# Attention scores on diagonal quarters of the array, one sign pass in two on DVE, and a third score buffer

## The chip, the cores and the metric

The kernel runs on one core of a Trainium2 chip. The metric is the time of one launch in device microseconds. Engines are TensorE (PE, with its weight loads PEld), VectorE (DVE), ScalarE (ACT), GpSimd (POOL) and SyncE (SP), which issues most of the DMAs. Each engine works through its own instructions in the order in which the program has them; semaphores tie the engines together.

## The reference

Three layers in a row, on 4 batches of 576 positions and a width of 512.

```python
# 1 attention: 8 heads of 64; heads 0-3 local, heads 4-7 strided
scores = np.matmul(q, k.transpose(0, 1, 3, 2)) / sqrt(64)
mask_local = (rel >= 0) & (rel < 32)
mask_strided = (rel >= 0) & (pos_k % 32 == pos_q % 32)
attn = softmax(where(mask, scores, -1e9));  x = attn @ v
# 2 layer norm and a dense layer, w_ch1 512x2048, w_ch2 2048x512
x = x + np.maximum(xn @ w_ch1, 0.0) @ w_ch2
# 3 one of 8 experts for each token (first layer 512x1024, second 1024x512)
out = p[e] * (np.maximum(x @ w1[e], 0) @ w2[e])
```

The weights of the second layer arrive as 64-bit floats; the kernel makes 32-bit floats of them by bit operations. A softmax row of a local head has 32 keys at most, one of a strided head 18, so only a band of the scores is computed.

## The kernel before

**Stages.** A prologue (to 57 us) computes the attention of batch 0 in an order written out by hand. Then comes a long row of steps of the dense layer, nine chunks of 256 tokens with 16 steps each (to about 615 us); the attention of batches 1, 2 and 3 is spread over its steps 6 to 24, 36 to 54 and 65 to 86, and the first 32 steps alternate between chunks 0 and 1. In those 32 steps the remaining weights are also split. The experts follow.

**Attention.** Two heads are a pair. `prep` transposes queries and keys of a pair on TensorE and copies them to SBUF. Keys lie as kT: 64 rows of head 0 over 64 rows of head 1. Queries lie as qbd: twice as wide, column 2s holds head 0 of position s in rows 0-63 and zeros below, column 2s+1 zeros above and head 1 in rows 64-127. So each half of the rows is copied on its own: in batch 0 the upper one by ACT and the lower one by DVE, later the lower one of the second half by ACT too. A unit is three or four groups of queries (64 for local pairs, 54 for strided ones). `st_scores` makes one product a group, 128 rows by 128 (or 108) query columns as weights against 96 (or 54) keys. In batches 0 and 1 a bf16 product first writes the mask into the bank. Then come the exponentials (ACT), the sum and scaling (DVE), `st_trans` (TensorE transposes, ACT copies to pt) and `st_out` (products with v; each head writes one half of the output partitions, into ps_o). The rows of a unit's scores alternate between the heads, and `st_out` reads every second column of pt. The scaled scores sm have two buffers (SMB) in batches 1 to 3. Of the 48 units 24 are local with three groups, 16 strided with four and 8 strided with three.

**Weights.** The dense layer's weights come in 32 pieces of 128 x 512 values (`load_w`). A piece takes five passes: `w_low` shifts the low words (DVE), `w_sign` writes the sign into the low word and then takes the scaled magnitude of the high word (both ACT), `w_high` joins the two (DVE), and `w_split` makes a high and a low part (ACT and POOL). Consecutive turns do them for consecutive pieces: in turn i the first pass of piece i, the second of piece i-1 and the split of piece i-2. Piece i < 6 (W_START) is worked on in the prologue, the rest in the steps of the dense layer. The calls through `keep` stay in program order; the other order of each engine is the scheduler's, by its own costs.

In the profile an operation of the prologue has line 84, whatever its place in the code. Lines used below: 324 scores, 374 transposes of sm, 382 copy to pt, 392 products with v, 290 to 294 queries, 288 keys, 454 `w_low`, 460 and 461 `w_sign`, 466 `w_high`, 480 and 481 `w_split`, 636 and 638 the first product of a step and its relu h, 639 the remainder of h, 652 the second product.

Of the kernel before, what the change touches and what calls it, by code (L numbers as in the profile page):

```python
# [22 lines left out]
B, H, S, DH = 4, 8, 576, 64  # L23
# [3 lines left out]
STR = 32  # L27
NA = S // STR
# [3 lines left out]
NTT = CT // TT  # L32
WL = 128 + NE + 1
QT = 96
SP = S + 18
GROUPS = (((0, 3), (3, 3), (6, 3)),) * 2 + (((0, 4), (4, 4), (8, 3)),) * 2
QW, KW = (64, 64, 54, 54), (96, 96, 54, 54)
SMW, PTW = 288, 432
# [4 lines left out]
SCALE = 1.0 / DH ** 0.5  # L43
NEG = -1.0e9
Z_THR = -1.5 * 2.0 ** -23


SMB, SM0, PT0, TL = 2, 4, 2, 1
WARM0, WARM, LB = 10, 5, 5
ORD = (((0, 1, 2), (0,)), ((3, 4, 5), (1,)), ((6, 7), (2,)))  # L50
SPANS = ((6, 24), (36, 54), (65, 86))
# [2 lines left out]
W_START, WR, WA, WI, W_DVE = 6, 1.3, 3, 5, 4  # L54
# [16 lines left out]
def attention_moe_moe(ctx: ExitStack, tc: tile.TileContext, q, k, v, g_ln, w_ch1, w_ch2, w_gate, w_local, w1, w2, out):  # L71
# [33 lines left out]
    pool.memset(mean_w, 1.0 / DM)  # L105
    mask_loc = cst.tile([128, 128], F32, name="mask_loc")
    pool.memset(mask_loc, 0.0)
    pool.affine_select(out=mask_loc, in_=mask_loc, pattern=[[-2, 128]], compare_op=ALU.is_ge, fill=-NEG, base=2 * STR, channel_multiplier=1)
    pool.affine_select(out=mask_loc, in_=mask_loc, pattern=[[2, 128]], compare_op=ALU.is_ge, fill=-NEG, base=-1, channel_multiplier=-1)
    mask_str = cst.tile([128, 3, NA], F32, name="mask_str")  # L110
    pool.memset(mask_str, 0.0)
    pool.affine_select(out=mask_str, in_=mask_str, pattern=[[-2 * NA, 3], [-2, NA]], compare_op=ALU.is_ge, fill=-NEG, base=0, channel_multiplier=1)
    pool.affine_select(out=mask_str, in_=mask_str, pattern=[[2 * NA, 3], [0, NA]], compare_op=ALU.is_ge, fill=-NEG, base=2 * NA - 1, channel_multiplier=-1)
    mask_str = mask_str.rearrange("p a b -> p (a b)")

    def high(ap):
# [36 lines left out]
    at_p = at_x.enter_context(tc.tile_pool(name="at_p", bufs=1))  # L153
# [20 lines left out]
        return ps_s["r"].tile(shape, F32, tag="s", name=name)  # L174


    qbds, kTs = [at_p.tile([128, SP, 2], F32, name="qbd")], [at_p.tile([128, SP], F32, name="kT")]
    spare = new_blk([128, 2048], F32, "spare")
    idle = spare[:, 1792:2048].bitcast(BF16)
    qbds.append(spare[:, 0:2 * SP].rearrange("p (s j) -> p s j", j=2))  # L180
    kTs.append(spare[:, 2 * SP:3 * SP])
    for qbd, kT in zip(qbds, kTs):
        pool.memset(qbd[0:64, :, 1], 0.0)
        pool.memset(qbd[64:128, :, 0], 0.0)
        pool.memset(qbd[0:64, S:SP, 0], 0.0)
        pool.memset(qbd[64:128, S:SP, 1], 0.0)
        pool.memset(kT[:, S:SP], 0.0)
    nat, vt, qTs = {}, {}, {}
    xts = {}

# [79 lines left out]
    def prep(b, hp, nm):  # L270

        odd = b == 0 and pairs.index((b, hp)) % 2
        qbd, kT = qbds[odd], kTs[odd]
        qTs[b, hp] = qbd, kT
        for half in range(2):
            t = nat.pop((nm, b, hp, half))
            ps = (ps_m.tile([128, 512], F32, tag="m", name="ps_tr")[:, 0:3 * QT] if b == 0 else side_r([128, 3 * QT], "ps_tr"))
            for i in range(3):
                pe.transpose(ps[:, QT * i:QT * i + QT], t[0:QT, i, :, :].rearrange("p h d -> p (h d)"), ident[0:QT, 0:QT])

            def dst(ap):
                if hp < 2:
                    return ap[:, 3 * QT * half:3 * QT * half + 3 * QT]
                return ap.rearrange("p (r a) -> p r a", a=NA)[:, :, NA // 2 * half:NA // 2 * half + NA // 2]

            s_ = ps if hp < 2 else ps.rearrange("p (a r) -> p r a", r=STR)
            if nm == "k":
                (act.copy if b == 0 else dve.tensor_copy)(dst(kT[:, 0:S]), s_)
            else:
                act.activation(dst(qbd[0:64, 0:S, 0]), s_[0:64], AF.Copy, scale=-SCALE)  # L290
                if half and b:
                    act.activation(dst(qbd[64:128, 0:S, 1]), s_[64:128], AF.Copy, scale=-SCALE)
                else:
                    dve.tensor_scalar(dst(qbd[64:128, 0:S, 1]), s_[64:128], -SCALE, None, op0=ALU.mult)

    sms, pts = {}, {}
    first, units = [], [0, 0]
# [5 lines left out]


    def shape_of(hp, u0):
        return dict(GROUPS[hp])[u0], QW[hp], KW[hp], 2 * QW[hp]

    def mode_of(b, hp):
        return MODES.get((b, hp), MODES.get(b, 0))

    def st_scores(b, hp, u0):
        ng, w, n, m = shape_of(hp, u0)
        ps = side([128, ng, n], "ps_sc")
        qbd, kT = qTs[b, hp]
        mode = mode_of(b, hp)
        mask = lambda i: mask_str[0:m, 0:n] if hp > 1 else mask_loc[:, STR:STR + n] if u0 + i == 0 else mask_loc[:, 0:n]
        if mode:
            cuts = [(0, 1), (1, ng)] if hp < 2 and u0 == 0 else [(0, ng)]
            for lo, hi_ in cuts:
                pe.matmul(ps[0:m, lo:hi_, :], high(ident[0:m, 0:m]), high(mask(lo)).unsqueeze(1).to_broadcast([m, hi_ - lo, n]), start=(lo == 0), stop=False)  # L320
        for i in range(ng):
            q0 = w * (u0 + i)
            k0 = max(0, q0 - STR) if hp < 2 else q0
            pe.matmul(ps[0:m, i, :], qbd[:, q0:q0 + w, :].rearrange("p s j -> p (s j)"), kT[:, k0:k0 + n], start=not mode, stop=not mode or i == ng - 1)  # L324
        if b == 0:
            k = units[0] % SM0 * SMW
            sm = first[0][:, k:k + ng * n]
            units[0] += 1
        else:
            sm = at_p.tile([128, SMW], F32, tag="sm", bufs=SMB, name="sm")[:, 0:ng * n]  # L330
        sm = sm.rearrange("p (g n) -> p g n", g=ng)
        st = at_p.tile([128, 2, 4], F32, tag="st", bufs=5, name="st")
        sms[b, hp, u0] = (sm, st, ps)
        mn = st[0:m, 0, 0:ng]
        if mode:
            new = [lambda: dve.tensor_reduce(mn, ps[0:m], axis=AX.X, op=ALU.min)]
            if mode == 1:
                new.append(lambda: dve.tensor_tensor(sm[0:m], ps[0:m], mn.unsqueeze(2).to_broadcast([m, ng, n]), op=ALU.subtract))
# [30 lines left out]
    def st_trans(b, hp, u0):  # L369
        sm, st, ps = sms.pop((b, hp, u0))  # L370
        ng, w, n, m = shape_of(hp, u0)
        ps = side([128, ng, m], "ps_pt")
        for i in range(ng):
            pe.transpose(ps[0:n, i, :], sm[0:m, i, :], ident[0:m, 0:m])
        if b == 0:
            k = SM0 * SMW + units[1] % PT0 * PTW
            pt = first[0][:, k:k + ng * m]
            units[1] += 1
        else:
            pt = at_p.tile([128, PTW], F32, tag="pt", bufs=2, name="pt")[:, 0:ng * m]  # L380
        pt = pt.rearrange("p (g m) -> p g m", g=ng)
        act.copy(pt[0:n], ps[0:n])
        pts[b, hp, u0] = pt

    def st_out(b, hp, u0):
        ng, w, n, m = shape_of(hp, u0)
        pt, vv = pts.pop((b, hp, u0)), vt.pop((b, hp, u0))
        ps = side([128, ng, w], "ps_o")
        for i in range(ng):
            k = min(w, S - w * (u0 + i)) if hp > 1 else w  # L390
            for j in range(2):
                pe.matmul(ps[64 * j:64 * j + 64, i, 0:k], vv[0:min(n, k) if hp > 1 else n, i, j, :], pt[0:min(n, k) if hp > 1 else n, i, j:2 * k:2], start=True, stop=True)
        o = ps.rearrange("p g q -> p (g q)")
        i = 0
        q0 = w * u0
        nq = min(w * ng, S - q0)
        for c in range(S * b // CT, (S * b + S - 1) // CT + 1):
            base = S * b - CT * c
            if hp < 2:
# [47 lines left out]
    def keep(ins):  # L447

        tc.keep_in_program_order(ins)

    def w_low(i):

        t = stage[i]
        keep(dve.tensor_single_scalar(t[..., 0], t[..., 0], 29, op=ALU.logical_shift_right))  # L454

    def w_sign(i):


# [501 lines left out]
    for n in range(2):  # L960
        i = n * (NE + 129)
# [526 lines left out]
```

## Time and profile before

| | |
|---|---|
| median of 3 runs | 904.97 us (904.07 to 905.69) |
| profiled execution | 902.98 us, its span 901.2 us |
| mean granted clock of TensorE | 0.983 |
| TensorE busy | 867.3 us, 96% of the span |
| DVE, ACT, POOL busy | 474.5, 365.6, 152.2 us |
| prologue / first 32 steps / later steps / experts | to 57 / to about 199 / to about 615 / to the end |

The span is the time from the first to the last instruction. Busy time is that in which an engine executes; a busy TensorE may still work at the lower of its two clock levels, so its busy time is to be read with the granted clock (1.00 is 2.4 GHz). Idle time counts only on the engine that others wait for. The name behind an arrow is the engine whose work ended the wait.

### The profile page before, as it was taken

The numbers are of one execution on the slowest core, as the hardware profiler recorded it, in microseconds if no ns is written. First come the engines' busy times: TensorE is split into PE (matmuls) and PEld (weight loads), VectorE is DVE, ScalarE is ACT, GpSimd is POOL, SyncE is SP. The second block draws the span as 40 slices with busy tenths as digits, with TensorE's granted clock in tenths as the row PEclk, the third lists the DMA queues.
The fourth block names the chain that finished last, engine by engine and source line by source line (L and its number), as shares of the span: only waits on it lengthen the run. The fifth ranks groups of instructions, "written<-read, shape, count | busy, mean of one in ns | idle before, by whom it ended". The sixth has DMA issues, their size and how long they took to land. (4 is left out here: it accounts for less than half of the span.)

```text
span 901.2 us, 17965 instructions
## 1 busy us (share of the span) xinstructions
PE 867.3 (96%) x6668; PEld 777.3 (86%) x6668; DVE 474.5 (53%) x1520; ACT 365.6 (41%) x879; POOL 152.2 (17%) x163
## 2 busy tenths in 40 slices
PE   8989888999999999999999999999999999999995
PEld 5769788999999999999999999999878787787763
DVE  4877775448766546666545555667521233111541
ACT  3688878433455234354211212332122334223550
POOL 2124323211120120120201212020231211110100
PEclk9999999899999999999999999999999999999997
DMA  9836244101212102211000000510663466410730
GB/s 190 250 106 207 59 141 121 50 14 52 65 39 46 48 10 64 47 26 39 1 1 25 1 25 6 207 49 24 239 225 101 150 218 215 139 37 24 291 113 15
DMA packets 95023, 82.91 MB, mean 92 GB/s; under 512 B 67395, under 2 KB 75589, under 8 KB 94920
## 3 DMA queue, kind: packets, MB, share of 16 engines
q1 hardware_dynamic: 87656, 65.41, 24.5%
q0 software_dynamic: 3632, 11.11, 3.7%
q10 hardware_dynamic: 3632, 5.09, 1.6%
q8 instruction: 55, 0.90, 0.4%
q14 instruction: 48, 0.39, 0.1%
HBM read 72.08 MB, written 10.30 MB: 91 GB/s over the span
## 5 line engine op out<-in xcount | busy, mean ns | idle before, releaser
L652 PE MATMUL acc<-h,w 128*128 128x256 f32 x1728 | 247.5, 291 | 1.6 <-DVE h L639 1.5
L636 PE MATMUL ps_h<-xc,w 128*128 128x256 f32 x1728 | 239.6, 287 | 0.0
L652 PEld LDWEIGHTS acc<-h,w 128*128 128x128 f32 x1728 | 220.7, 192 | 5.1 <-DVE h L639 2.5
L636 PEld LDWEIGHTS ps_h<-xc,w 128*128 128x128 f32 x1728 | 221.6, 194 | 1.7
L638 ACT ACTIVATE h<-ps_h 128x256 fp32r<-128x256 f32 x144 | 55.6, 387 | 218.3 <-PE ps_h L636 203.7
L639 DVE SCALAR_TENSOR_TENSOR h<-ps_h,h 128x256 fp32r<-128x256 f32 x144 | 60.6, 421 | 94.2 <-ACT h L638 93.5
L1367 PE MATMUL ps_h<-wx,xs 128*128 128x512 f32 x360 | 87.6, 398 | 0.8 <-DVEq L1294 0.8
L1395 PE MATMUL ps_y<-wx,ht 128*128 128x512 f32 x360 | 87.5, 399 | 0.0
L1367 PEld LDWEIGHTS ps_h<-wx,xs 128*128 128x128 f32 x360 | 66.6, 188 | 15.8 <-DVEq L1294 1.2
L1395 PEld LDWEIGHTS ps_y<-wx,ht 128*128 128x128 f32 x360 | 67.6, 191 | 13.8
L481 POOL TENSOR_TENSOR w<-stg,w 128x512 fp32r<-128x512 f32 x32 | 45.6, 1424 | 120.7 <-ACT w L480 74.5
L1398 ACT ACTIVATE y<-ps_y,pr 128x512 f32<-128x512 f32 x19 | 13.1, 687 | 90.5 <-PE ps_y L1395 54.9
L890 DVE TENSOR_TENSOR xs<-ps_tx,xs 128x512 fp32r<-128x512 f32 x15 | 10.4, 691 | 63.0 <-ACTq L1294 44.8
L1370 ACT ACTIVATE h<-ps_h 128x512 f32<-128x512 f32 x30 | 16.3, 595 | 60.8 <-PE ps_h L1367 60.8
L782 DVE TENSOR_TENSOR wx<-raw,wx 128x1024 fp32r<-128x1024 f32 x32 | 37.5, 1220 | 1.7 <-ACT wx L779 1.3
L460 ACT ACTIVATE stg<-stg 128x512 f16<-128x512 f32 x27 | 37.2, 1377 | 0.6 <-DVE stg L454 0.6
L1399 POOL DMA_INDIRECT out_dram<-y,idx x15 | 15.1, 1007 | 114.6 <-ACT y L1398 66.1
L779 ACT CAST wx<-raw 128x1024 fp32r<-128x1024 f32 x32 | 31.8, 1061 | 5.7 <-PE acc L652 4.1
L354 ACT ACTIVATE sm<-sm,st 108x54 f32<-108x54 f32 (+1 forms) x80 | 27.6, 347 | 13.5 <-DVE st L342 13.4
L1384 DVE TENSOR_TENSOR ht<-ps_th,ht 128x512 fp32r<-128x512 f32 x30 | 19.3, 685 | 24.5 <-ACT ht L1383 24.1
L324 PE MATMUL ps_sc<-kT,qbd 128*108 128x54 f32 (+1 forms) x240 | 30.5, 267 | 0.0
L892 DVE SCALAR_TENSOR_TENSOR pr<-io_e,e_rep,xg 128x8 f32<-128x8 f32 x15 | 3.4, 226 | 51.2 <-ACT y L1398 46.0
(393 smaller groups left out, 1233.7 us busy)
## 6 DMA issues: line engine op xcount, KB each, us to landing
stg<-in_moe_w_ch_dram SPq DMA_DIRECT2D x32, 512.0 KB
raw<-in_moe_w_dram SPq DMA_DIRECT2D x16, 1024.0 KB
raws<-in_moe_w_dram SPq DMA_DIRECT2D x16, 1024.0 KB
xrows<-row ACTq DMA_DIRECT2D x9, 520.0 KB
qnat<-in_q_dram SPq DMA_DIRECT2D x48, 72.0 KB
knat<-in_k_dram SPq DMA_DIRECT2D x48, 72.0 KB
v<-in_v_dram SPq DMA_DIRECT2D x24, 72.0 KB
v<-in_v_dram SPq DMA_DIRECT2D x72, 18.0 KB
```

The costliest lines, as they stand in the source:

```text
L324: pe.matmul(ps[0:m, i, :], qbd[:, q0:q0 + w, :].rearrange("p s j -> p (s j)"), kT[:, k0:k0 + n], start=not mode, stop=not mode or i == ng - 1)
L354: act.activation(sm[0:m, i, :], (ps if mode else sm)[0:m, i, :], AF.Exp, bias=st[0:m, 0, i:i + 1], scale=-1.0, **({} if mode else dict(acc ...
L460: keep(act.activation(t.bitcast(F16)[..., 1], f32(t[..., 1]), AF.Copy, scale=2.0 ** -112))
L481: keep(pool.tensor_tensor(w[:, 1], r, f32(w[:, 0]), op=ALU.subtract))
L636: pe.matmul(ps, w[:, a, d, o:o + 128], xcs[c][:, b_, d, :], start=(i == 0), stop=(i == 11))
L638: act.activation(h[:, 0, :], ps, AF.Relu)
L639: dve.scalar_tensor_tensor(h[:, 1, :], ps, 0.0, f32(h[:, 0, :]), op0=ALU.max, op1=ALU.subtract)
L652: pe.matmul(accs[c][d // 2][:, d % 2, :], w[:, a, f % 2, d * 128:(d + 1) * 128], h[:, b_, :], start=(f == 0 and (a, b_) == (0, 0) and d % ...
L779: act.copy(wx[i][:, 0, :], raw[i // 2][:, i % 2, :])
L782: dve.tensor_tensor(wx[i][:, 1, :], raw[i // 2][:, i % 2, :], f32(wx[i][:, 0, :]), op=ALU.subtract)
L1367: pe.matmul(hp_[fg], s_[:, a, d, :], wx[d][:, b_, 512 * fg:512 * fg + 512], start=(i == 0), stop=(i == 11))
L1395: pe.matmul(ps, s_[a][:, f, :], wx[4 + f // 2][:, b_, 512 * (f % 2):512 * (f % 2) + 512], start=(i == 0), stop=(i == 23))
```

## The change

Queries are kept as qT, like the keys, without zeros: one copy for both heads, by DVE in batch 0 and by ACT later. The score product of a group becomes two, one for each head, with 64 rows and 64 weight columns each: head 0 on the upper left quarter of the array, head 1 on the lower right one. The scores' rows are then head 0 (0-63) and head 1 (64-127), also for strided pairs, which had 108 rows before; masks are built by halves, the copy to pt leaves out the columns without a query, and `st_out` reads pt without a stride. For pieces 6, 8, ... 30 the sign is joined by DVE right after `w_low`, and ACT's first pass is gone. SMB is 3.

```diff
-SP = S + 18
+SP = S + 32
-SMB, SM0, PT0, TL = 2, 4, 2, 1
+SMB, SM0, PT0, TL = 3, 4, 2, 1
...
+    for j in range(2):
+        m = mask_loc[64 * j:64 * j + 64, :]
+        pool.affine_select(out=m, in_=m, pattern=[[-1, 128]], compare_op=ALU.is_ge, fill=-NEG, base=STR, channel_multiplier=1)
...
-    for qbd, kT in zip(qbds, kTs):
-        pool.memset(qbd[0:64, :, 1], 0.0)
...
-        pool.memset(kT[:, S:SP], 0.0)
+    for ab in qks:
+        for t in ab:
+            pool.memset(t[:, S:SP], 0.0)
...
             if nm == "k":
                 (act.copy if b == 0 else dve.tensor_copy)(dst(kT[:, 0:S]), s_)
+            elif b == 0:
+                dve.tensor_scalar(dst(qT[:, 0:S]), s_, -SCALE, None, op0=ALU.mult)
             else:
-                act.activation(dst(qbd[0:64, 0:S, 0]), s_[0:64], AF.Copy, scale=-SCALE)
-                if half and b:
-                    act.activation(dst(qbd[64:128, 0:S, 1]), s_[64:128], AF.Copy, scale=-SCALE)
-                else:
-                    dve.tensor_scalar(dst(qbd[64:128, 0:S, 1]), s_[64:128], -SCALE, None, op0=ALU.mult)
+                act.activation(dst(qT[:, 0:S]), s_, AF.Copy, scale=-SCALE)
...
-    return dict(GROUPS[hp])[u0], QW[hp], KW[hp], 2 * QW[hp]
+    return dict(GROUPS[hp])[u0], QW[hp], KW[hp], 128
...
-            pe.matmul(ps[0:m, i, :], qbd[:, q0:q0 + w, :].rearrange("p s j -> p (s j)"), kT[:, k0:k0 + n], start=not mode, stop=not mode or i == ng - 1)
+            for j in range(2):
+                h = slice(64 * j, 64 * j + 64)
+                pe.matmul(ps[h, i, :], qT[h, q0:q0 + 64], kT[h, k0:k0 + n], start=not mode, stop=not mode or i == ng - 1)
...
-        act.copy(pt[0:n], ps[0:n])
+        act.copy(pt[0:n], ps[0:n].rearrange("p g (j q) -> p g j q", j=2)[:, :, :, 0:w])
...
+    def sign_dve(i):
+        return i >= W_START and i % 2 == 0
+
     def w_low(i):
         t = stage[i]
         keep(dve.tensor_single_scalar(t[..., 0], t[..., 0], 29, op=ALU.logical_shift_right))
+        if sign_dve(i):
+            keep(dve.scalar_tensor_tensor(t[..., 0], t[..., 1], -2 ** 31, t[..., 0], op0=ALU.bitwise_and, op1=ALU.bitwise_or))
...
-        keep(act.activation(t.bitcast(F16)[..., 1], f32(t[..., 1]), AF.Copy, scale=2.0 ** -112))
+        if not sign_dve(i):
+            keep(act.activation(t.bitcast(F16)[..., 1], f32(t[..., 1]), AF.Copy, scale=2.0 ** -112))
         keep(act.activation(f32(t[..., 1]), f32(t[..., 1]), AF.Abs, scale=2.0 ** -112))
```

What this does to the order of TensorE at the second unit of batch 0: before, the mask, the three score products of whole width and the transposes of the next pair.

```order
L84 LDWEIGHTS iw
L84 MATMUL ps_sc<-mask_loc,iw 128x288
L84 MATMUL ps_sc<-kT,qbd 128x96 x3
L84 MATMUL ps_tr<-iw,qk 128x96 x6
L84 LDWEIGHTS spare
```

And the same place of TensorE with the change.

```order
L84 LDWEIGHTS iw
L84 MATMUL ps_sc<-mask_loc,iw 128x288
L84 MATMUL ps_sc<-kT,qT 64x96 x6
L84 MATMUL ps_tr<-iw,qk 128x96 x6
L84 LDWEIGHTS spare
```

Nothing moves there but the three products, which are six of half the height. The second place is ACT between two casts of the weights of the dense layer, where the pieces alternate (w_2 and w_3 are split weights); first before.

```order
L480 CAST w_2_915<-stg 128x4x128
L460 ACTIVATE stg<-stg 128x512
L638 ACTIVATE h<-ps_h 128x256
L461 ACTIVATE stg<-stg 128x512
L480 CAST w_2_1002<-stg 128x512
L460 ACTIVATE stg<-stg 128x512
L461 ACTIVATE stg<-stg 128x512
L638 ACTIVATE h<-ps_h 128x256
L480 CAST w_3_1109<-stg 128x4x128
```

ACT with the change, at the same weights.

```order
L484 CAST w_2_953<-stg 128x4x128
L464 ACTIVATE stg<-stg 128x512
L465 ACTIVATE stg<-stg 128x512
L642 ACTIVATE h<-ps_h 128x256
L484 CAST w_2_1041<-stg 128x512
L465 ACTIVATE stg<-stg 128x512
L484 CAST w_3_1147<-stg 128x4x128
```

One cast in two is followed by two passes on stg as before, the other by one. The third place is DVE at the first softmax steps of batch 1: before, four passes on stg (454 and 466) stand among these rows.

```order
L639 SCALAR_TENSOR_TENSOR h<-ps_h,h 128x256
L466 SCALAR_TENSOR_TENSOR stg<-stg 128x512 x2
L454 TENSOR_SCALAR stg<-stg 128x512
L639 SCALAR_TENSOR_TENSOR h<-ps_h,h 128x256
L336 TENSOR_REDUCE st<-ps_sc 128x3
L338 TENSOR_TENSOR sm<-ps_sc,st 128x288
L466 SCALAR_TENSOR_TENSOR stg<-stg 128x512
L366 TENSOR_REDUCE st<-sm 128x3
```

DVE with the change, at the same steps; line 457 is the join of the sign.

```order
L643 SCALAR_TENSOR_TENSOR h<-ps_h,h 128x256
L286 COPY kT<-ps_tr 128x288 x2
L470 SCALAR_TENSOR_TENSOR stg<-stg 128x512
L455 TENSOR_SCALAR stg<-stg 128x512
L457 SCALAR_TENSOR_TENSOR stg<-stg 128x512
L334 TENSOR_REDUCE st<-ps_sc 128x3
L643 SCALAR_TENSOR_TENSOR h<-ps_h,h 128x256
L470 SCALAR_TENSOR_TENSOR stg<-stg 128x512
L336 TENSOR_TENSOR sm<-ps_sc,st 128x288
```

The join stands behind the shift of its piece (455), and the first reduction of the scores now stands ahead of a relu remainder instead of behind it.

## Rows read from the trace of the kernel before

**Rows 1.** Stretches: length, busy of PE, PEld, DVE, ACT, POOL, clock, DMA
```profile
60.00:180.00 120.00, 110.11 (x918) 103.80 (x917) 83.12 (x199) 91.11 (x159) 38.64 (x29) 0.91 0.38 110
200.00:600.00 400.00, 398.60 (x3569) 390.37 (x3568) 244.91 (x931) 141.45 (x464) 51.35 (x48) 1.00 0.14 40
...
60.00:80.00 20.00, 20.00 (x152) 19.36 (x151) 18.63 (x39) 18.02 (x31) 7.62 (x6) 0.91 0.34 100
```

**Rows 2.** Waits of TensorE, 60 to 200 us: total, times, longest
```profile
PE ps_pt L374 <- DVE sm L363: 2.3, 1, 2.3
PE ps_o L392 <- ACT pt L382: 1.8, 2, 1.0
PE ps_tr L279 <- ACT pt L382: 1.2, 1, 1.2
PE ps_tr L279 <- ACT qbd L292: 0.9, 2, 0.7
PE ps_o L392 <- PE ps_o L392: 0.9, 1, 0.9
PE ps_pt L374 <- ACT xt L410: 0.8, 2, 0.5
PE acc L652 <- DVE h L639: 0.8, 2, 0.6
PE ps_tr L279 <- DVE qbd L294: 0.8, 2, 0.6
PE ps_var L572 <- ACT pt L382: 0.4, 1, 0.4
```

**Rows 3.** ACT in order of time, 118 to 121 us: start, duration
```profile
118.33 1.38 ACT L460 ACTIVATE stg<-stg 128x512 f16<-128x512 f32 x1
...
120.38 0.45 ACT L382 COPY pt<-ps_pt 96x384 f32<-96x384 f32 x1
```

**Rows 4.** Groups by line: busy us, mean ns, idle before
```profile
L460 ACT ACTIVATE stg<-stg 128x512 f16<-128x512 f32 x27 | 37.2, 1377 | 0.6 <-DVE stg L454 0.6
L466 DVE SCALAR_TENSOR_TENSOR stg<-stg 128x512 int32<-128x512 int32 x27 | 18.6, 689 | 11.1 <-ACT stg L461 10.7
L290 ACT ACTIVATE qbd<-ps_tr 64x288 f32<-64x288 f32 x24 | 9.5, 441 | 0.6 <-PE ps_tr L279 0.6
L294 DVE TENSOR_SCALAR qbd<-ps_tr 64x288 f32<-64x288 f32 x12 | 5.6, 463 | 1.4 <-ACT qbd L290 1.2
```

**Rows 5.** TensorE in the prologue, score blocks and what follows
```profile
10.59 0.80 PE L84 MATMUL ps_sc<-kT,qbd 128*128 128x96 f32 x6
11.23 0.66 PE L84 MATMUL ps_tr<-iw,qk 96*128 96x96 f32 x6
11.73 1.46 PE L84 MATMUL idle_ps<-spare 128*128 128x512 bf16 x6
...
17.93 0.93 PE L84 MATMUL ps_sc<-spare 128*108 128x54 f32 x8 [1.55 <-ACT spare L84]
...
20.82 0.88 PE L84 MATMUL ps_sc<-spare 128*108 128x54 f32 x8
21.54 0.49 PE L84 MATMUL ps_pt<-iw,first 128*96 128x128 f32 x3
```

**Rows 6.** TensorE, blocks of ps_o and ps_pt and what follows
```profile
18.70 0.49 PE L84 MATMUL ps_pt<-iw,first 128*96 128x128 f32 x3
19.13 0.57 PE L84 MATMUL ps_o<-first,v 96*64 96x64 f32 x12
19.63 1.25 PE L84 MATMUL idle_ps<-spare 128*128 128x512 bf16 x5
...
112.86 0.49 PE L374 MATMUL ps_pt<-iw,sm 128*96 128x128 f32 x3
113.19 0.29 PE L320 MATMUL ps_sc<-mask_loc,iw 128*128 128x288 bf16 x1
...
253.36 0.92 PE L392 MATMUL ps_o<-pt,v 96*64 96x64 f32 x24
254.21 1.70 PE L636 MATMUL ps_h<-xc,w 128*128 128x256 f32 x12
```

More of the change, by code (lines that the diff above doesn't have):

```diff
@@ L107, in attention_moe_moe @@
     pool.memset(mask_loc, 0.0)
-    pool.affine_select(out=mask_loc, in_=mask_loc, pattern=[[-2, 128]], compare_op=ALU.is_ge, fill=-NEG, base=2 * STR, channel_multiplier=1)
-    pool.affine_select(out=mask_loc, in_=mask_loc, pattern=[[2, 128]], compare_op=ALU.is_ge, fill=-NEG, base=-1, channel_multiplier=-1)
     mask_str = cst.tile([128, 3, NA], F32, name="mask_str")
     pool.memset(mask_str, 0.0)
-    pool.affine_select(out=mask_str, in_=mask_str, pattern=[[-2 * NA, 3], [-2, NA]], compare_op=ALU.is_ge, fill=-NEG, base=0, channel_multiplier=1)
-    pool.affine_select(out=mask_str, in_=mask_str, pattern=[[2 * NA, 3], [0, NA]], compare_op=ALU.is_ge, fill=-NEG, base=2 * NA - 1, channel_multiplier=-1)
+    for j in range(2):
+        m = mask_loc[64 * j:64 * j + 64, :]
+        pool.affine_select(out=m, in_=m, pattern=[[-1, 128]], compare_op=ALU.is_ge, fill=-NEG, base=STR, channel_multiplier=1)
+        pool.affine_select(out=m, in_=m, pattern=[[1, 128]], compare_op=ALU.is_ge, fill=-NEG, base=-1, channel_multiplier=-1)
+        m = mask_str[64 * j:64 * j + 64]
+        pool.affine_select(out=m, in_=m, pattern=[[-NA, 3], [-1, NA]], compare_op=ALU.is_ge, fill=-NEG, base=0, channel_multiplier=1)
+        pool.affine_select(out=m, in_=m, pattern=[[NA, 3], [0, NA]], compare_op=ALU.is_ge, fill=-NEG, base=NA - 1, channel_multiplier=-1)
     mask_str = mask_str.rearrange("p a b -> p (a b)")
@@ L174, in side_r @@
         return ps_s["r"].tile(shape, F32, tag="s", name=name)
-    qbds, kTs = [at_p.tile([128, SP, 2], F32, name="qbd")], [at_p.tile([128, SP], F32, name="kT")]
+    qks = [(at_p.tile([128, SP], F32, name="qT"), at_p.tile([128, SP], F32, name="kT"))]
     spare = new_blk([128, 2048], F32, "spare")
     idle = spare[:, 1792:2048].bitcast(BF16)
-    qbds.append(spare[:, 0:2 * SP].rearrange("p (s j) -> p s j", j=2))
-    kTs.append(spare[:, 2 * SP:3 * SP])
-    for qbd, kT in zip(qbds, kTs):
-        pool.memset(qbd[0:64, :, 1], 0.0)
-        pool.memset(qbd[64:128, :, 0], 0.0)
-        pool.memset(qbd[0:64, S:SP, 0], 0.0)
-        pool.memset(qbd[64:128, S:SP, 1], 0.0)
-        pool.memset(kT[:, S:SP], 0.0)
+    qks.append((spare[:, 0:SP], spare[:, SP:2 * SP]))
+    for ab in qks:
+        for t in ab:
+            pool.memset(t[:, S:SP], 0.0)
     nat, vt, qTs = {}, {}, {}
@@ L272, in prep @@
         odd = b == 0 and pairs.index((b, hp)) % 2
-        qbd, kT = qbds[odd], kTs[odd]
-        qTs[b, hp] = qbd, kT
+        qT, kT = qTs[b, hp] = qks[odd]
         for half in range(2):
@@ L313, in st_scores @@
         ps = side([128, ng, n], "ps_sc")
-        qbd, kT = qTs[b, hp]
+        qT, kT = qTs[b, hp]
         mode = mode_of(b, hp)
@@ L376, in st_trans @@
             k = SM0 * SMW + units[1] % PT0 * PTW
-            pt = first[0][:, k:k + ng * m]
+            pt = first[0][:, k:k + 2 * ng * w]
             units[1] += 1
         else:
-            pt = at_p.tile([128, PTW], F32, tag="pt", bufs=2, name="pt")[:, 0:ng * m]
-        pt = pt.rearrange("p (g m) -> p g m", g=ng)
-        act.copy(pt[0:n], ps[0:n])
+            pt = at_p.tile([128, PTW], F32, tag="pt", bufs=2, name="pt")[:, 0:2 * ng * w]
+        pt = pt.rearrange("p (g j q) -> p g j q", g=ng, j=2)
+        act.copy(pt[0:n], ps[0:n].rearrange("p g (j q) -> p g j q", j=2)[:, :, :, 0:w])
         pts[b, hp, u0] = pt
@@ L391, in st_out @@
             for j in range(2):
-                pe.matmul(ps[64 * j:64 * j + 64, i, 0:k], vv[0:min(n, k) if hp > 1 else n, i, j, :], pt[0:min(n, k) if hp > 1 else n, i, j:2 * k:2], start=True, stop=True)
+                pe.matmul(ps[64 * j:64 * j + 64, i, 0:k], vv[0:min(n, k) if hp > 1 else n, i, j, :], pt[0:min(n, k) if hp > 1 else n, i, j, 0:k], start=True, stop=True)
         o = ps.rearrange("p g q -> p (g q)")
```

## The prediction

> **What bounds the kernel now.** I read the stretches of time first, then the waits of TensorE, then the groups by line, and the order in time last. The two long stretches [rows 1] show what limits each half of the program. From 200 to 600 us TensorE is busy for 398.6 of 400 us at full clock. Whatever is added to its stream there is added to the time, and nothing that ACT or DVE saves there is worth anything. From 60 to 180 us, where the first weights are split while the products of chunks 0 and 1 and the attention of batch 1 run, it is different: TensorE is busy for 110.1 of 120 us and its granted clock is 0.91 on average. So 9.9 us are idle, and 120 x 0.09 = 10.8 us of full-speed work are lost to the clock, which in those spells is at the lower of its levels, 1.2 instead of 2.4 GHz. Together 20.7 us are lost there. This is the only place of the first half in which a faster ACT can pay.
>
> Who causes it is in the waits of TensorE [rows 2]. Those that name ACT (pt twice, qbd, xt, ps_var) sum to 1.8 + 1.2 + 0.9 + 0.8 + 0.4 = 5.1 us; those that name DVE (sm, h, qbd) to 2.3 + 0.8 + 0.8 = 3.9 us; one wait on an output bank is 0.9 us. The reader can see one of them in the order of ACT [rows 3]: the copy of pt at 120.38, for which TensorE waits 1.0 us, stands behind a sign pass of 1.38 us that began at 118.33, a relu and a second weight pass. ACT is busy for 91.1 and DVE for 83.1 us of that stretch [rows 1]; each is in order, so a product waits for whatever weight pass stands ahead of its copy.
>
> **The sign joined by DVE.** Pieces 6, 8, ..., 30 are 13 pieces; piece 30 is split after 180 us, so 12 lie in the stretch. ACT loses 12 x 1.377 = 16.5 us [rows 4]. DVE gains 12 instructions of the form of line 466, which has the same shape and types, at 0.689 us: 8.3 us [rows 4]. The new instruction stands right behind the shift of the same piece on DVE and adds no wait on another engine; queued behind it are the relu remainders h, the softmax steps and the joins of other pieces, and the products and ACT's casts wait for those. The query preparation of batch 1 (four pairs) falls from three ACT passes and one DVE pass on half the partitions to two ACT passes on all: ACT minus 4 x 0.44 = 1.8 us, DVE minus 4 x 0.46 = 1.8 us [rows 4]. ACT then has 91.1 - 18.3 = 73 us of work, DVE 83.1 + 6.5 = 90 of 120: the two change places, but the fuller one is no fuller than ACT was. Of the 5.1 us behind ACT I take two thirds as gone, 3.4 us, and 0.6 of the bank wait, which follows the same copies; the 3.9 us behind DVE stay. That is 4.0 us. The clock loss came after such gaps, so I let half of it go, 5.4 us. Sum: minus 9. The bounds are nothing (DVE's lateness replaces ACT's) and all 20.7 us; above zero it can go as far as DVE's 6.5 us all on the path.
>
> **The scores on quarters.** A product was one fp32 matmul in two passes; it becomes two, on rows and columns 0-63 and 64-127, so four passes. How the old block is paced: three groups of 96 columns take from 10.59 to 11.23 = 0.64 us, four groups of 54 from 20.82 to 21.54 = 0.72 us [rows 5]; I take 0.54 for three groups of 54, three quarters of it. No row has a product on 64 rows, so the price comes from the nearest rows, ps_o, whose two heads already lie on column halves. Six pairs take 0.50 us (19.13 to 19.63), twelve pairs 0.85 (253.36 to 254.21) [rows 6]: 0.058 us a pair of passes, so the halves overlap, and 0.15 us fixed. Ahead of it, three transposes last 0.43 us before a ps_o block (18.70 to 19.13) and 0.33 before a mask product (112.86 to 113.19) [rows 6]: another 0.10 us on entry. So leaving and entering the whole array costs 0.25 us a block. A pair with 54 columns goes at 0.058 as in ps_o; one with 96 columns cannot go faster than its columns stream, 0.083 us, which the transposes with 96 columns show (six from 11.23 to 11.73) [rows 5]. The new blocks are then 0.25 + 6 x 0.083 = 0.75 (before 0.64), 0.25 + 8 x 0.058 = 0.71 (0.72) and 0.25 + 6 x 0.058 = 0.60 (0.54). There are 24, 16 and 8 of them: 24 x 0.11 - 16 x 0.01 + 8 x 0.06 = plus 2.9 us. The passes are fewer columns wide, and yet the block is not shorter. From below, if 96 columns went at 0.058 too, the sum is minus 0.7 us; from above, if the two quarters of a pair took turns, it is plus 25 (a rival below).
>
> What stands between quarters and halves is that quarters also differ in rows. The row is ps_o, where halves with the same rows overlap [rows 6]. The Trainium skill (TensorEngine Tiling (Array Packing), Restrictions and Gotchas) says that different row tiles must not access the same PSUM bank at one time; both quarters here write one bank, in different partitions. By that rule the pairs would take turns; no run here shows a row tile.
>
> The strided heads now fill 128 rows instead of 108, so their 88 transposes stream 128 columns: 0.110 us each [rows 6] against 108/128 of that, 0.093: plus 1.5 us. Masks, reductions and exponentials act on more partitions but as many elements in each: no change. The product with pt reads it contiguously instead of every second element; the pace of 0.058 is the same for 64 and 54 columns, so I take nothing. TensorE's sum is plus 4.4 us, of which 200 to 600 us pays its half in full.
>
> **The prologue.** The query copies leave ACT and are one DVE pass per half. At 17.93 TensorE waited 1.55 us for ACT, which copied keys late because query passes and exponentials stood ahead [rows 5]. Two passes of 0.44 leave its queue and DVE no longer waits for their turn: minus 1.5 us, with 0 and 2.5 as ends. GpSimd has four more selects and six fewer memsets in its first microseconds, all beside the warm-up products: nothing.
>
> **Three buffers for sm.** No row names a wait for a free sm: TensorE's wait is for its contents [rows 2]. I take nothing, with up to 1 us either way since the scheduler reorders the softmax steps.
>
> **Sum.** -9 + 4.4 - 1.5 = -6.1 us. The profiled execution took 902.98 us (span 901.2 and 1.78 around it); the median of the runs is 904.97, which is 2.0 higher, so I apply the difference to the median: 904.97 - 6.1 = 898.9, rounded to 899.
>
> **Rivals.** (1) Nearly all of the loss goes, because clock spells are steps: with few gaps none begins. Of 20.7 us, 17 go: -17 + 4.4 - 1.5 = -14, 891. For it: ACT's load falls by a fifth, and six of nine waits stand behind ACT or its copies [rows 2]. Against: the longest, 2.3 us, names DVE.
> (2) DVE takes ACT's place, slower. DVE is already busy for 18.6 of the 20 us from 60 to 80 [rows 1]; three joins there, 2.1 us, less one query pass, 0.5, fill it past 20. From there its queue runs late, h and sm reach TensorE late, the waits change their name and the clock spells stay: 4.4 - 1.5 + about 1 us = +4, 909. It decides where DVE's share over the stretch passes what ACT had, 91 of 120; my sum is 90.
> (3) The quarters take turns, slower. Blocks of 0.25 + 12 x 0.083 = 1.25, 0.25 + 16 x 0.058 = 1.18 and 0.25 + 12 x 0.058 = 0.95 cost 24 x 0.61 + 16 x 0.46 + 8 x 0.41 = 25 instead of 2.9: -6.1 + 22 = +16, 921. The overlap in ps_o speaks against it; that its halves share rows leaves it open.
> (4) The parts cancel: 4 to 5 us recovered against 4.4 on TensorE less the prologue: within 2 us, 904.
>
> **How the numbers follow.** Forecast (-11 to -2 us) 0.48, rival 1 0.17, rival 2 0.14, rival 3 0.10, rival 4 0.11. A measurement can tell about 0.2%, 1.8 us, from no change. Faster: 0.48 + 0.17 and a little of rival 4, 0.67; same 0.11; slower 0.22, with the slow edge of rival 4 inside it. The likeliest case alone spans 894 to 903. The range for 8 in 10 leaves out rival 3 and the far end of rival 1: 889 to 909.
>
> **What would show it.** A score block in the new trace: 0.75 us for 96 columns and a pair step of 0.083 says right; 1.2 says rival 3. Between 60 and 180 us: ACT near 73 and DVE near 90 us busy, idle of TensorE near 6 us and a granted clock near 0.95. A clock of 0.91 with waits that name DVE is rival 2; a clock of 0.99 is rival 1. From 200 to 600 us the same work must end about 2 us later than it began later. The wait at 17.93 must be gone. Wrong above all would be the forecast if clock spells fall elsewhere by chance of where a gap lies, since each is several us.

## The result and the profile after

The changed kernel takes 897.36 us (median of 7 runs, 896.54 to 899.08). The kernel before, run beside it, took 904.07 us (7 runs, 900.58 to 906.34). The ratio is 0.9911 with a 95% interval of 0.9889 to 0.9934: faster by 0.9%. The profiled execution took 896.78 us, its span 894.9; mean granted clock 0.992, before 0.983. The forecast was 899 us; most of its parts were not what moved the time.

The stretches of the profile after (length, busy time and count of PE, PEld, DVE, ACT and POOL, granted clock, DMA share, GB/s) answer to [rows 1]:

```profile
60.00:180.00 120.00, 110.07 (x1048) 101.17 (x1048) 93.17 (x209) 71.96 (x141) 37.34 (x28) 0.97 0.40 111
200.00:600.00 400.00, 398.44 (x3713) 384.63 (x3713) 238.43 (x922) 135.59 (x447) 50.23 (x47) 1.00 0.15 42
60.00:80.00 20.00, 18.02 (x145) 17.05 (x145) 19.72 (x41) 13.75 (x25) 7.55 (x6) 1.00 0.39 125
```

From 60 to 180 us ACT fell from 91.1 to 72.0 us and DVE rose from 83.1 to 93.2, the forecast's swap. TensorE is as idle as before: 9.9 us in either. What changed is the clock, 0.91 before and 0.97 now: 120 x 0.03 = 3.6 us of full-speed work lost where it was 10.8. The waits of TensorE, 60 to 200 us (total, times, longest), answer to [rows 2]:

```profile
PE acc L656 <- DVE h L643: 2.2, 3, 0.9
PE ps_o L390 <- issue: 1.3, 1, 1.3
PE ps_tr L277 <- ACT pt L380: 1.3, 1, 1.3
PE ps_sc L316 <- DVE sm L336: 1.1, 1, 1.1
PE ps_o L390 <- DVE sm L336: 0.8, 1, 0.8
PE ps_pt L372 <- DVE sm L361: 0.7, 1, 0.7
PE ps_sc L316 <- DVE xt L408: 0.6, 1, 0.6
PE ps_h L640 <- DVE xc L624: 0.6, 1, 0.6
PE ps_sc L316 <- DVE kT L286: 0.5, 1, 0.5
PE ps_o L390 <- DVE kT L286: 0.5, 1, 0.5
PE ps_var L576 <- ACT pt L380: 0.2, 1, 0.2
```

The names moved from ACT to DVE (ACT 5.1 to 1.5 us, DVE 3.9 to 7.0), the sum did not: 9.8 us here, 9.9 there. The two waits that named copies of queries (qbd) have no successor. The longest wait fell from 2.3 to 1.3 us.

Where the 6.3 us of the span (901.2 to 894.9) arise is read from three instructions of TensorE that both programs have: the first dense product, the last ps_rs of the weights' steps, and the first block of ps_tx. In order of time, after (start, duration):

```profile
54.40 3.42 PE L640 MATMUL ps_h<-xc,w 128*128 128x256 f32 x24
...
192.04 0.59 PE L614 MATMUL ps_rs<-dg,mean_w 128*128 128x256 f32 x2
...
601.90 1.03 PE L880 MATMUL ps_tx<-iw,xg 128*128 128x128 f32 x8
```

And before:

```profile
56.91 3.41 PE L636 MATMUL ps_h<-xc,w 128*128 128x256 f32 x24
...
198.56 0.59 PE L610 MATMUL ps_rs<-dg,mean_w 128*128 128x256 f32 x2
...
607.58 1.04 PE L876 MATMUL ps_tx<-iw,xg 128*128 128x128 f32 x8
```

The prologue ends 2.5 us earlier; the weights' steps take 137.6 instead of 141.7 (-4.0); the later steps 409.9 instead of 409.0 (+0.8); the rest 293.0 instead of 293.6 (-0.6). Sum -6.3. In the prologue the granted clock is 1.00 in both, so its 2.5 us have nothing to do with the clock. In the weights' steps the time falls by less than the 7.2 us of lost work that are gone there.

### The profile page after: what moved, and what is told of

Read it like the earlier page. It is cut to its first block, busy times and chain, and to the rows that moved or that the text cites. A ratio compares the mean times of both kernels' runs of the same rounds, so it can differ in the third digit from the quotient of the medians.

```text
span 894.9 us, 18582 instructions
## 1 busy us (share of the span) xinstructions
PE 864.6 (97%) x6988; PEld 764.3 (85%) x6988; DVE 483.0 (54%) x1521; ACT 341.2 (38%) x846; POOL 149.3 (17%) x161
## 5 line engine op out<-in xcount | busy, mean ns | idle before, releaser
L640 PE MATMUL ps_h<-xc,w 128*128 128x256 f32 x1728 | 235.9, 285 | 0.6 <-DVE xc L624 0.6
L640 PEld LDWEIGHTS ps_h<-xc,w 128*128 128x128 f32 x1728 | 218.6, 192 | 2.5 <-DVE xc L624 0.9
L352 ACT ACTIVATE sm<-sm,st 128x54 f32<-128x54 f32 (+1 forms) x80 | 27.6, 347 | 13.2 <-DVE st L340 13.1
L1399 PE MATMUL ps_y<-wx,h2t 128*128 128x512 f32 x96 | 24.2, 400 | 1.7 <-DVE h2t L1129 1.7
L873 POOL DMA_INDIRECT xg<-xrows,idx x16 | 16.3, 1020 | 56.0 <-PE ps_y L1399 27.6
```

Source lines behind the costliest of these rows:

```text
L352: act.activation(sm[0:m, i, :], (ps if mode else sm)[0:m, i, :], AF.Exp, bias=st[0:m, 0, i:i + 1], scale=-1.0, **({} if mode else dict(acc ...
L640: pe.matmul(ps, w[:, a, d, o:o + 128], xcs[c][:, b_, d, :], start=(i == 0), stop=(i == 11))
L873: pool.indirect_dma_start(out=x, out_offset=None, in_=xrows[0:n], in_offset=bass.IndirectOffsetOnAxis(ap=places(s)[0], axis=0), bounds_che ...
L1399: pe.matmul(ps, s_[a][:, f, :], wx[4 + f // 2][:, b_, 512 * (f % 2):512 * (f % 2) + 512], start=(i == 0), stop=(i == 23))
```

## The experiments

Every run lists its mean granted clock, so the work lost to the clock, (1 - clock) x span, can be averaged over all runs of a kernel. One profiled execution is a poor witness: the changed kernel shows 0.97 from 60 to 180 us above, and 0.94 in another execution (e7). Medians and ratios against the kernel before, run on the same chip (906.81 beside e1 to e4, 906.05 beside e5 to e8, 904.83 beside e9 to e12):

| kernel | us (runs) | ratio, 95% interval | mean clock | lost, us |
|---|---|---|---|---|
| before | 904 to 907 | 1 | 0.981 to 0.983 | 15.3 to 17.5 |
| after | 897.36 (7) | 0.9911, 0.9889 to 0.9934 | 0.991 | 8.5 |
| e1 sign alone | 902.00 (12) | 0.9958, 0.9938 to 0.9977 | 0.989 | 10.1 |
| e2 all but the sign | 895.75 (6) | 0.9896, 0.9871 to 0.9922 | 0.992 | 7.5 |
| e3 two buffers | 897.53 (6) | 0.9911, 0.9886 to 0.9935 | 0.990 | 9.0 |
| e4 head by head | 904.68 (10) | 0.9977, 0.9960 to 0.9993 | 0.992 | 6.9 |
| e6 quarters alone | 904.33 (12) | 0.9983, 0.9964 to 1.0002 | 0.986 | 12.5 |
| e7 after, once more | 897.25 (5) | 0.9912, 0.9879 to 0.9944 | 0.990 | 8.8 |
| e8 all signs by DVE | 895.87 (6) | 0.9892, 0.9862 to 0.9922 | 0.991 | 7.9 |
| e9 e2, batch 0 split | 896.25 (6) | 0.9901, 0.9882 to 0.9920 | 0.992 | 7.0 |
| e10 e2, batches 1-3 split | 899.62 (6) | 0.9934, 0.9912 to 0.9957 | 0.990 | 9.4 |
| e11 after, all split | 900.52 (10) | 0.9952, 0.9934 to 0.9970 | 0.989 | 10.3 |
| e12 e8, keys by ACT | 900.22 (6) | 0.9948, 0.9929 to 0.9967 | 0.987 | 11.5 |

Time less loss is between 888 and 892 us for every kernel but e4 (898), whose products are slower. That makes the loss look like the whole difference, but it isn't a sum in time. In the 55 runs of the kernel before, 1 us more of loss goes with only about 0.5 us more of time. Its six runs with a clock of 0.990 or 0.991 take 900.3 to 903.1 us, while the three runs of the changed kernel with 0.991 (two of the result, one of e7) take 896.5 to 898.2. So the clock is one part of what the kernels differ in, and at the same clock a difference remains; how the two share it is not settled here. ("Split" means query copies by halves of the partitions, as before.)

**The parts alone.** The theory was the prediction's: the sign, by way of ACT, is the main term.

e1, the kernel before with `sign_dve` for the even pieces (the same lines as in the change, nothing else). Expected:

> The kernel before, with the sign of every second piece joined by DVE and nothing else changed. If the gain comes from ACT's relief in the weights' stretch (my theory), the time falls by 4 to 7 us against before (897 to 900), the granted clock from 60 to 180 us rises above 0.95 and ACT is busy for about 75 us there; the wait of 1.55 us at 17.9 us stays. If the gain comes from the one-pass query copies and their prologue (rival), it stays within 1.5 us of before.

e2, the changed kernel without it:

```diff
     def sign_dve(i):
-        return i >= W_START and i % 2 == 0
+        return False
```

> The changed kernel with both sign passes on ACT again for all pieces: quarters, one-pass query copies and three buffers remain. My theory: the prologue keeps its 2.5 us, the quarters cost about 1 us in the later steps, and the weights' stretch is as lossy as before (idle near 10 us, clock near 0.91), so 902 to 904, which is 5 us or more above the changed kernel. Rival (copies and quarters bring it): 897 to 899, like the changed kernel.

e3, `SMB` back to 2:

> The changed kernel with two buffers for scaled scores instead of three. My theory: no wait was for a free buffer, so within 1 us of the changed kernel (897.4). If the third buffer is what lets DVE run ahead, 2 us or more slower, with TensorE waits for sm that grow.

The theory falls with e2: 895.75, no slower than the whole change. Its stretch:

```profile
60.00:180.00 120.00, 109.44 (x1058) 100.65 (x1058) 81.46 (x198) 87.92 (x157) 38.38 (x29) 0.99 0.39 112
```

ACT is nearly as full as before (87.9 of 120, before 91.1), TensorE is idle for 10.6 us, and yet the clock is 0.99. A full ACT was not what made the loss. By itself the sign does help the kernel before (e1, -0.4%): its stretch has a clock of 0.97 with ACT busy for 76.7 us, as expected of it, and the time is 4.8 us lower. e3 shows nothing for the third buffer.

**The order of the quarters.** e4 exchanges the loops of the score products, all groups of one head first:

```diff
-        for i in range(ng):
...
-            for j in range(2):
+        for j in range(2):
+            for i in range(ng):
```

> The changed kernel with the quarter products of a unit in the order all of head 0, then all of head 1, so that neighbours lie on the same quarter of the array and cannot overlap. If the pairs overlap in the changed kernel because they lie on different rows and columns, a block of three 96-column groups takes about 1.2 us instead of 0.73 and one of four 54-column groups 1.15 instead of 0.69; 24 units of the later steps then cost about 11 us more there, and some 15 to 22 us in all: 912 to 920. If neighbours on one quarter overlap as well (weights of the next loaded beside the running one), under 3 us more.

The prologue of e4 on TensorE (start, duration, tile, operation), a local block, then a strided one with four groups:

```profile
10.20 0.93 PE L84 MATMUL ps_sc<-kT,qT 64*64 64x96 f32 x12
11.06 0.71 PE L84 MATMUL ps_tr<-iw,qk 96*128 96x96 f32 x6
...
16.38 0.94 PE L84 MATMUL ps_sc<-spare 64*64 64x54 f32 x16
17.26 0.53 PE L84 MATMUL ps_pt<-iw,first 128*96 128x128 f32 x3
```

The blocks take 0.86 and 0.88 us, where the changed kernel takes 0.64 and 0.60 (below). So passes of neighbouring products on the two quarters do run beside each other, and the alternation is needed for all of it. The kernel is 7.3 us slower than the changed one; the size expected was too high, since the runs of the two heads still overlap where they meet.

**The query copies.** A copy in one pass is what e2 still had and the sign did not explain. e5 is the kernel before with one copy a half, on its full-width products; head 1's queries are left out (zeros in their place):

```diff
-        pool.memset(qbd[64:128, S:SP, 1], 0.0)
+        pool.memset(qbd[64:128, :, 1], 0.0)
...
-                act.activation(dst(qbd[0:64, 0:S, 0]), s_[0:64], AF.Copy, scale=-SCALE)
-                if half and b:
-                    act.activation(dst(qbd[64:128, 0:S, 1]), s_[64:128], AF.Copy, scale=-SCALE)
+                if b == 0:
+                    dve.tensor_scalar(dst(qbd[0:64, 0:S, 0]), s_[0:64], -SCALE, None, op0=ALU.mult)
                 else:
-                    dve.tensor_scalar(dst(qbd[64:128, 0:S, 1]), s_[64:128], -SCALE, None, op0=ALU.mult)
+                    act.activation(dst(qbd[0:64, 0:S, 0]), s_[0:64], AF.Copy, scale=-SCALE)
```

> The kernel before with one query copy a half instead of two: head 1's queries are left out (zeros stand in their place), the products keep their whole width, signs and buffers are as before. What is left for ACT and DVE is as in the changed kernel. If the one-pass copies bring the gain, the prologue ends 2 us earlier (first product of the dense layer near 54.5 instead of 56.9 us), the mean clock of a run rises from 0.981 to above 0.988 and the time falls by 6 us or more against before; if the quarters or the new order bring it, the prologue's 1.5 to 2 us remain as the only gain.

Its total (960.91 us) can't be compared: other attention values send the tokens to other experts. Up to the experts the work is the same, and its three marks are:

```profile
54.19 3.41 PE L635 MATMUL ps_h<-xc,w 128*128 128x256 f32 x24
...
189.98 0.59 PE L609 MATMUL ps_rs<-dg,mean_w 128*128 128x256 f32 x2
...
599.40 1.03 PE L875 MATMUL ps_tx<-iw,xg 128*128 128x128 f32 x8
```

By the last it is 8.2 us ahead of the kernel before, 2.7 from the prologue and 5.9 from the weights' steps (the later steps take 0.4 more), with neither quarters nor sign. This compares one execution with one: the weights' steps of the changed kernel take 137.6 us above and 139.9 in e7. e6 is the opposite, the changed kernel without the sign and with the old copies (only `qT` in place of `qbd`):

```diff
-            elif b == 0:
-                dve.tensor_scalar(dst(qT[:, 0:S]), s_, -SCALE, None, op0=ALU.mult)
             else:
-                act.activation(dst(qT[:, 0:S]), s_, AF.Copy, scale=-SCALE)
+                act.activation(dst(qT[0:64, 0:S]), s_[0:64], AF.Copy, scale=-SCALE)
+                if half and b:
+                    act.activation(dst(qT[64:128, 0:S]), s_[64:128], AF.Copy, scale=-SCALE)
+                else:
+                    dve.tensor_scalar(dst(qT[64:128, 0:S]), s_[64:128], -SCALE, None, op0=ALU.mult)
...
-        return i >= W_START and i % 2 == 0
+        return False
```

> The changed kernel without the sign join and with the query copies split over two passes on half the partitions, as before: quarters, three buffers, 128 rows and the order that follows remain. If the quarters keep the clock up, the mean clock is 0.990 or more and the time 896 to 899; if the one-pass copies did, the clock falls back to about 0.981 and the time lies at or above that of before, by 1 us for the longer blocks.

e6 takes the time of the kernel before again, a ratio of 0.9983 whose interval reaches 1. Its stretch:

```profile
60.00:180.00 120.00, 108.76 (x985) 100.20 (x984) 81.25 (x198) 89.21 (x158) 38.34 (x28) 0.91 0.39 110
```

And three of its waits of TensorE, the first in the prologue, the others from 60 to 200 us:

```profile
PE ps_sc L84 <- ACT spare L84: 1.2, 1, 1.2
...
PE ps_sc L318 <- DVE sm L338: 2.8, 1, 2.8
...
PE ps_tr L277 <- ACT qT L290: 1.1, 2, 0.9
```

In this execution the clock of 0.91 is back, and so are the prologue's wait for ACT and waits that name the copies of queries. Over all runs the mean clock is 0.986, between before (0.983 beside it) and e2 (0.992): of the 8.6 us between the medians of e6 and e2, 5.0 are loss, and the rest is not.

e7 is the changed kernel once more, beside these; e8 takes the sign of all pieces from 6 on to DVE (`return i >= W_START`).

> The changed kernel as it is, on the same chip as the other three and beside before, to compare them: 0.991 of before, as in its first comparison.

> The changed kernel with the sign of all pieces from 6 on joined by DVE: 13 more joins of 0.69 us on DVE and 13 more sign passes of 1.38 us off ACT. The kernel without any join was 1.6 us faster than the changed one by medians. If DVE's lateness is what a join costs, all joins are slower still: DVE busy above 100 of 120 us from 60 to 180 us, 2 to 5 us above the changed kernel. If ACT's relief is what counts, equal or faster.

e8 was to show whether DVE becomes the bound. Its stretch, and its longest waits of TensorE from 60 to 200 us:

```profile
60.00:180.00 120.00, 109.90 (x1050) 100.98 (x1050) 101.79 (x221) 58.29 (x130) 41.38 (x29) 0.97 0.38 111
```

```profile
PE ps_sc L316 <- DVE kT L286: 3.9, 2, 3.3
...
PE ps_o L390 <- DVE kT L286: 1.3, 2, 0.8
```

With DVE busy for 101.8 of 120 us and one wait of 3.3 us behind it the kernel is as fast as the changed one. The expectation that made DVE's load decisive did not hold, and e2, with ACT nearly full, is as fast, so ACT's relief isn't decisive either.

**Which copies, and their sum with the sign.** e9 splits the copies of batch 0 alone, e10 those of batches 1 to 3 alone, both on e2; e11 splits all of them in the changed kernel, sign on DVE. e12 is e8 with the keys of batches 1 to 3 copied by ACT, against the wait of 3.3 us:

```diff
-                (act.copy if b == 0 else dve.tensor_copy)(dst(kT[:, 0:S]), s_)
+                act.copy(dst(kT[:, 0:S]), s_)
```

> The kernel with quarters and no sign join (0.990 of before), its query copies split over ACT and DVE again in batch 0 alone. Theory now: the one-pass copies bring the gain, since a bank of ps_tr is given back after one pass instead of after two on engines that are both late. If batch 0 carries only its part of the prologue, the first product of the dense layer comes 2 us later (56.3 instead of 54.3 us) and the time rises by 2 us, to 0.992 of before; the mean clock stays at 0.991. If the phase of the later stretch is what counts, the clock falls to 0.986 and the gain goes altogether.

> The same kernel, its query copies split again in batches 1 to 3 alone. If the copies of batch 1 inside the weights' stretch keep the clock up, this loses the larger part, 5 to 6 us: 0.996 of before, mean clock 0.986, idle time of TensorE behind qT and pt, while the prologue still ends at 54.3 us. If it is the prologue that shifts everything, it stays at 0.990 to 0.992.

> The changed kernel (sign of every second piece by DVE) with all query copies split as before. It completes the square of copies and signs. If the sign join helps only where the copies are split, as before with the join alone (0.996) and the changed kernel without it (0.990) suggest, it lies near 0.996, with a mean clock of 0.989; if the two parts add, near 0.998 or above.

> All signs from piece 6 on joined by DVE (0.989 of before), and the keys of batches 1 to 3 copied by ACT instead of DVE. With all signs on DVE, 5.2 of its 10 us of waits between 56 and 200 us name the keys' copies on DVE, which was busy for 102 of 120 us there, ACT for 58. If those waits cost time, they go and 1 to 4 us are won: 892 to 895, faster than the changed kernel. If the clock decides, equal within 1 us.

e6, e11, e2 and e7 are the four corners of copies and sign, all on quarters (intervals of a difference: the half widths, squared, added, and the root):

| ratio | sign by ACT | sign by DVE | difference |
|---|---|---|---|
| copies split | 0.9983 | 0.9952 | -0.31% (± 0.26) |
| copies in one pass | 0.9896 | 0.9912 | +0.16% (± 0.41) |
| difference | -0.87% (± 0.32) | -0.40% (± 0.37) | |

The one-pass copy is worth 7.9 us without the sign on DVE and 3.6 with it; both are clear of the noise. The sign is worth 2.8 us where copies are split (3.8 by e1, on the products of the kernel before) and nothing that can be measured where they are not. That the two gains overlap is likely, not certain: the differences differ by 0.47% (± 0.49). Of the 0.87% the copies of batches 1 to 3 carry 0.38% (e10 against e2, ± 0.34), those of batch 0 0.05% (e9, ± 0.32); the two do not add up to the whole, at the edge of what the intervals allow. e9's first dense product starts at 56.93, e10's at 54.38: the prologue's 2.5 us belong to the copies of batch 0. Yet e9 is only 0.5 us above e2. With an interval of ± 2.9 us that doesn't tell whether a later start of the dense layer is lost in full.

e12 missed (892 to 895 had been expected). The kT waits are gone, and these two lead its list:

```profile
PE ps_pt L372 <- DVE sm L361: 3.4, 1, 3.4
PE ps_sc L316 <- DVE sm L336: 2.0, 1, 2.0
```

A wait of 3.3 us was exchanged for one of 3.4 under another name, and the loss rose from 7.9 to 11.5 us.

## Why the prediction came out right, and where it was wrong

**The time.** -6.1 us was forecast, -6.7 measured by the medians, inside the likeliest case (894 to 903).

**The step that failed is "the sign joined by DVE, minus 9".** Both halves of its reasoning fail. The idle time was to fall by 4.0 us since TensorE waited for ACT; it fell by 0.1. The waits changed their names, as rival 2 had it, but at no cost that the runs can measure; DVE was busy for 19.7 of the 20 us from 60 to 80, as rival 2 feared, and the clock there was 1.00. The clock loss was to fall by 5.4 and fell by 7.2 in the profiled execution (7 to 9 in the mean of all runs), but e2 has that without the sign. Nor is a microsecond of loss a microsecond of time, as the sum has it: the weights' steps became 4.0 us shorter. The sign's own worth is 2.8 to 3.8 us where copies are split, and nothing that can be measured in this company.

**The term too small: the query copies.** I had priced them at 1.5 us in the prologue, and for the later batches only as ACT's and DVE's time (1.8 us each). e5 and e6 show that they carry the change: 8.2 us to the experts without any other part, and nothing left when only they are undone along with the sign. [Rows 2] had the hint: two waits for qbd, one by each engine, 1.7 us, which I counted with their engines instead of with the operation. Before, the copies of a bank of transposed queries in batch 0, and of one half in the later batches, stood in the queues of two engines; now each stands in one. That this handover is how they act is argued from those waits (gone in e2 and after, 1.5 us in e6), not shown. A rival is left untested: the change also makes two passes into one, and no run separates the two. Each edit also lets the scheduler reorder other work.

**DVE's load, right in sign, too small.** DVE rose by 10.1 instead of 6.5 us. Its join has a mean of 844 ns, not 689, and `w_high` rose too (last section). No run shows a cost of it. Of the 13 joins 12 do start in the stretch; the one outside is that of piece 6, at 56.4, and not that of piece 30, at 156.1.

**The quarters: right.** The prologue after, mask, scores and what follows, for the three kinds of blocks:

```profile
10.17 0.29 PE L84 MATMUL ps_sc<-mask_loc,iw 128*128 128x288 bf16 x1
10.39 0.71 PE L84 MATMUL ps_sc<-kT,qT 64*64 64x96 f32 x12
11.03 0.71 PE L84 MATMUL ps_tr<-iw,qk 96*128 96x96 f32 x6
...
18.80 0.26 PE L84 MATMUL ps_sc<-mask_str,iw 128*128 128x216 bf16 x1
19.00 0.67 PE L84 MATMUL ps_sc<-spare 64*64 64x54 f32 x16
19.60 0.53 PE L84 MATMUL ps_pt<-iw,first 128*96 128x128 f32 x3
...
22.19 0.24 PE L84 MATMUL ps_sc<-mask_str,iw 128*128 128x162 bf16 x1
22.36 0.56 PE L84 MATMUL ps_sc<-spare 64*64 64x54 f32 x12
22.85 0.41 PE L84 MATMUL ps_pt<-iw,first 128*54 128x128 f32 x2
```

And where the masks of these blocks began before (what follows the first two, at 11.23 and 21.54, is in [rows 5]):

```profile
10.46 0.29 PE L84 MATMUL ps_sc<-mask_loc,iw 128*128 128x288 bf16 x1
...
20.72 0.26 PE L84 MATMUL ps_sc<-mask_str,iw 108*108 108x216 bf16 x1
...
24.10 0.24 PE L84 MATMUL ps_sc<-mask_str,iw 108*108 108x162 bf16 x1
...
24.71 0.54 PE L84 MATMUL ps_pt<-iw,first 108*54 108x108 f32 x4
```

From the mask's start to the next operation: 0.86, 0.80 and 0.66 us. The same stretches before are 0.77, 0.82 and 0.61. So 24 x 0.09 - 16 x 0.02 + 8 x 0.05 = +2.2, forecast +2.9. Taken from the first product, as the prediction took them, the blocks are 0.64, 0.60 and 0.49 us and not 0.75, 0.71 and 0.60: the 0.10 us of entry lies ahead of it, between mask and first product (0.22 us where it was 0.13 in the first block). A pair of passes takes 0.082 us with 96 columns and 0.058 with 54, by the starts of the single passes, as forecast. Rival 3 is refuted, by the pace here and by e4. The later steps pay +0.8 us where I had 2.2; part of the difference is that the blocks of ps_o come there in 12 pieces instead of 14, two fewer changes of 0.25 us.

**The prologue.** Right in kind (the wait of 1.55 us at 17.93 is gone), too small: -2.5 us net of the longer blocks, where the terms gave -1.5 + 1.1 = -0.4. The prediction saw only that wait. A later one, of the same transposes of scores, shrank too; before, then after:

```profile
48.28 0.53 PE L84 MATMUL ps_pt<-iw,first 128*96 128x128 f32 x3 [1.89 <-DMA stg<-in_moe_w_ch_dram]
...
45.79 0.53 PE L84 MATMUL ps_pt<-iw,first 128*96 128x128 f32 x3 [1.25 <-DVE first L84]
```

From 10 us to the first dense product the waits sum to 4.5 us before and 2.0 after.

**The third buffer: right**, nothing (e3).

**The sum.** It was right by luck: -9 for the sign stood where the copies' 4 to 8 us belong, and half of the clock loss was taken to go, for a reason that e2 refutes. Rival 1 went for the clock in the right direction and too far; rivals 2 and 4 did not come about.

**Open.** Why a given set of gaps lets the clock fall and another does not, and why 1 us of loss costs only about half a us. Idle time between 60 and 200 us, summed over the waits of one execution of each, is 9.9 us before, 9.8 after, 10.2 in e2, 9.8 in e8, 11.3 in e6, 11.8 in e10 and 11.2 in e12: the kernels that lose most have a little more than the others, but the kernel before loses most of all at 9.9. e8 and e12 have nearly the same longest wait (3.3 and 3.4 us) and differ by 3.6 us of loss; e2 has one of 2.2 us at a clock of 0.99. No kernel here beats the changed one for certain: e2 and e8 are 1.5 us lower, with intervals that overlap.

## What to carry to other kernels

A form of a product that lets one engine empty a bank in one pass can be worth more than the product itself costs: price the evacuation it permits as well. Where idle gaps are few and the clock is under 1, compare the clock over all runs, not the idle time of one profile, and then compare runs at the same clock before calling the clock the cause. When two edits aim at the same loss, undo them in a square of four; alone, each may be credited with what the other also gives.

## What the runs showed of the hardware

**Quarters in one bank overlap.** The Trainium skill (TensorEngine Tiling (Array Packing), Restrictions and Gotchas) says that different row tiles cannot access the same PSUM bank at one time. Here two products on different rows, writing different partitions of one bank, take 0.082 us as a pair with 96 columns. Head by head, neighbouring passes on one quarter begin 0.082 us apart each, and the block is 0.22 us longer. For diagonal quarters the measurement decides: they do not take turns.

**DVE passes stretch beside GpSimd.** In the changed kernel, DVE and POOL in order of time (start, duration):

```profile
130.07 1.32 DVE L470 SCALAR_TENSOR_TENSOR stg<-stg 128x512 int32<-128x512 int32 x1
...
150.20 1.74 DVE L457 SCALAR_TENSOR_TENSOR stg<-stg 128x512 int32<-128x512 int32 x1
```

```profile
129.52 1.32 POOL L485 TENSOR_TENSOR w<-stg,w 128x512 fp32r<-128x512 f32 x1 [3.58 <-ACT w L484]
...
150.07 1.31 POOL L485 TENSOR_TENSOR w<-stg,w 128x512 fp32r<-128x512 f32 x1 [2.21 <-ACT w L484]
```

A pass of 0.68 us that starts while POOL's tensor operation runs ends 0.55 us after it (131.39 after 130.84; 151.94 after 151.38; POOL's times are rough in the profile). The two groups by line (busy us, mean ns, idle before):

```profile
L470 DVE SCALAR_TENSOR_TENSOR stg<-stg 128x512 int32<-128x512 int32 x27 | 21.4, 792 | 7.0 <-ACT stg L465 6.7
L457 DVE SCALAR_TENSOR_TENSOR stg<-stg 128x512 int32<-128x512 int32 x13 | 11.0, 844 | 0.2
```

Seven of these 40 passes take over 1 us, each held in this way; of the 27 of `w_high` before none did (696 ns at most). So the mean of the join is 844 ns, and that of `w_high` rises from 689 to 792. A pass with one input can be held too: `w_low` took 1.49 us at 132.99, beside POOL's 132.88 to 134.18. The Trainium skill (GPSIMD Engine Reference, Specifications) says that the engine's SBUF interfaces are shared with VectorE, with contention where a DVE instruction has two SBUF inputs; the join has two, and the trace agrees.
